# Turning the strided q and k of five batches by DMA transposes instead of TensorE transposes

## The chip, the cores and the metric

One core of a Trainium2 chip runs the whole program. The metric is the device time of one execution in microseconds (us). Executions of one kernel scatter by about 1%; where two traces of one kernel exist, they differ only at the start, where the first weights arrive (shown below). Every execution told here was in the fast state, but for micro, a single run whose state is unknown.

In this program TensorE does the matmuls and writes them to banks of PSUM. ScalarE and VectorE do the softmax and copy ("evict") the banks to SBUF, the on-chip memory. GpSimd casts loaded tiles to 16 bits, and SyncE issues the loads and stores. A DMA transpose is a transfer that turns a matrix on its way.

## The reference

Eight batches of causal attention with eight heads of 64 and 576 tokens, then a multiplicative feed-forward part over all 4608 tokens:

```python
mask_local   = (rel >= 0) & (rel < 32)                 # heads 0..3
mask_strided = (rel >= 0) & (k_pos % 32 == q_pos % 32) # heads 4..7
attn = softmax(where(mask, q @ k.T / 8, -1e9)) @ v
x = attn.transpose(0, 2, 1, 3).reshape(4608, 512)
out = ((x @ w1) * (x @ w2) @ w3) @ w_out               # 512 -> 1024 -> 512
```

## The kernel before

It is recorded as a list of operations that a small scheduler in the kernel's source orders at build time; each engine then runs its list in order. w3 @ w_out is folded into one matrix `w34` at the start. After that, nine tiles of 512 tokens (ps_a, ps_b, ps_o: `x @ w1`, `x @ w2`, `... @ w34`) alternate with the attention of the batches ahead of them. Two heads make a head pair; pairs 0 and 1 are local, 2 and 3 strided.

Scores need q and k with the 64 head elements on the partitions. So 512 of the 576 tokens come in as 128 rows of 4 tokens, are cast by GpSimd, turned by TensorE (ps_T) and copied out of PSUM; the other 64 "rest" tokens come in extra and are turned by small matmuls (ps_R):

```python
def fnT(e, ...):                       # one head pair: q and k, 8 transposes
    for j, x in ((0, "q"), (1, "k")):
        ps = bank("f", key)[:, j]
        for c in range(4):
            nc.tensor.transpose(ps[:, c*P:(c+1)*P], x16[(b, x, hp // 2)][:, c, h0:h0 + 2]..., id16)
tp = plan.op(key, {"PE": 450}, fnT, ...)
def fe(e, i, ...):                     # two evictions: into qT, and into kTL (local) or kTS (strided)
    copy(e, o, ps.rearrange(...))
evs.append(plan.op(f"E{nm}{nm2}", {"ACT": 590, "DVE": 690}, fe, deps=[tp] + wr, ...))
...
plan = Plan(dict(f=NF, B=2, stg=NSTG, asb=2, osb=3, ...))   # f: four PSUM banks; osb: three output buffers
# output: ScalarE copies a PSUM bank into an osb buffer, SyncE stores it; the buffer is free when that has landed
```

The softmax here doesn't subtract the row's maximum and nothing guards it: scores larger than these inputs give would overflow.

## Time and profile before

| | before |
|---|---|
| time, median of 4 runs | 279.55 us (278.8 to 280.18) |
| span of the profiled execution | 277.2 us |
| TensorE / VectorE / ScalarE / GpSimd busy | 97 / 63 / 63 / 43% |
| period of a tile while attention runs beside | 27.23 us |

The prediction shows the main lines: TensorE has no gap between about 40 us and the end. Two groups of the page (busy us and mean ns of one, then idle time before and who ended it) are what the change removes in part:

```profile
L666 PE MATMUL ps_T<-id,x 128*128 128x128 f16 x256 | 19.5, 219 | 1.0 <-POOL x L308 0.8
L304 ACT COPY qT<-ps_T 128x512 f16<-128x512 f16 x16 | 9.4, 588 | 9.3 <-PE ps_T L666 9.3
```

The 256 transposes are 32 blocks of eight; ten blocks go. What a block costs is worked out in the prediction.

### The profile page before, as it was taken

The numbers are of one execution on the slowest core, as the hardware profiler recorded it, in microseconds if no ns is written. First come the engines' busy times: TensorE is split into PE (matmuls) and PEld (weight loads), VectorE is DVE, ScalarE is ACT, GpSimd is POOL, SyncE is SP. The second block draws the span as 40 slices with busy tenths as digits, with TensorE's granted clock in tenths as the row PEclk, the third lists the DMA queues.
The fourth block names the chain that finished last, engine by engine and source line by source line (L and its number), as shares of the span: only waits on it lengthen the run. The fifth ranks groups of instructions, "written<-read, shape, count | busy, mean of one in ns | idle before, by whom it ended". The sixth has DMA issues, their size and how long they took to land.

```text
span 277.2 us, 6298 instructions
## 1 busy us (share of the span) xinstructions
PE 268.5 (97%) x2433; PEld 150.8 (54%) x2433; DVE 173.6 (63%) x328; ACT 174.1 (63%) x321; POOL 117.9 (43%) x146
## 2 busy tenths in 40 slices
PE   7977999999999999999999999999999999999995
PEld 3556885656555555555555555555555544444443
DVE  6544577776778577857785778577767763320321
ACT  2862477847668775886588668856885775324321
POOL 6676987699969969450835082100000000000000
PEclk9999999999999999999999999999999999999999
DMA  7999999998999998977366200310030003003003
GB/s 245 338 361 273 344 357 359 264 267 272 362 280 276 322 297 298 257 245 234 114 163 229 85 4 0 115 40 2 1 116 38 2 24 127 4 0 151 0 2 151
DMA packets 53422, 48.65 MB, mean 175 GB/s; under 512 B 20752, under 2 KB 45584, under 8 KB 53392
## 3 DMA queue, kind: packets, MB, share of 16 engines
q1 hardware_dynamic: 53392, 48.24, 57.3%
q8 instruction: 19, 0.31, 0.5%
q14 instruction: 11, 0.09, 0.1%
HBM read 38.80 MB, written 9.44 MB: 174 GB/s over the span
## 4 chain that ended last, share of the span: by engine, by line
PE 91%; DMA 6%; POOL 2%; SPq 0%; DVE 0%; issue 0%; DVEq 0%
PE ps_o L897 23%; PE ps_b L877 23%; PE ps_a L861 22%; PE ps_T L666 5%; PE ps_mm L594 4%; PE ps_S L709 4%; DMA st<-in_moe_w_out_dram 3%; PE ps_X L757 3%; PE ps_X L747 3%; DMA st<-in_k_dram 3%; PE ps_U L826 2%; PE ps_tr L575 1%; PE ps_R L619 1%; SPq L311 0%; POOL x16r L308 0%; POOL woh L308 0%
## 5 line engine op out<-in xcount | busy, mean ns | idle before, releaser
L883 DVE TENSOR_TENSOR abt<-ps_b,asb 128x512 f16<-128x512 f32 x72 | 49.3, 689 | 39.3 <-PE ps_b L877 38.7
L877 PE MATMUL ps_b<-xT,w2h 128*128 128x512 f16 x288 | 73.8, 379 | 0.0
L861 PE MATMUL ps_a<-xT,w1h 128*128 128x512 f16 x288 | 73.8, 379 | 0.0
L304 ACT COPY asb<-ps_a 128x512 f32<-128x512 f32 x72 | 42.2, 589 | 40.2 <-PE ps_a L861 39.4
L897 PE MATMUL ps_o<-w,abt 128*128 128x512 f16 (+1 forms) x296 | 67.4, 374 | 0.0
L308 POOL CAST x<-st 128x1024 f16<-128x1024 f32 x32 | 32.8, 1037 | 31.6 <-PE ps_T L666 25.2
L877 PEld LDWEIGHTS <-w2h 128*128 128x128 f16 x288 | 26.9, 98 | 29.2
L897 PEld LDWEIGHTS <-abt 128*128 128x128 f16 x296 | 26.9, 98 | 27.7
L861 PEld LDWEIGHTS <-w1h 128*128 128x128 f16 x288 | 26.5, 99 | 26.5
L727 ACT ACTIVATE ps_S<-ps_S 96x576 f32<-96x576 f32 (+1 forms) x56 | 32.9, 628 | 11.0 <-PE ps_S L709 10.5
L304 ACT COPY osb<-ps_o 128x512 f32<-128x512 f32 x35 | 20.6, 588 | 18.4 <-PE ps_o L897 18.2
L813 DVE TENSOR_TENSOR xT<-ps_X,rcp 64x288 f16<-64x288 f32 x56 | 25.1, 448 | 5.9 <-ACT rcp L797 5.3
L308 POOL CAST v16L<-st 32x768 f16<-32x768 f32 (+1 forms) x32 | 26.3, 821 | 3.0 <-DMA st<-in_v_dram 1.3
L735 DVE TENSOR_TENSOR ptm<-ps_S,maskL 128x576 f16<-128x576 f32 x28 | 19.8, 750 | 12.2 <-ACT ps_S L727 12.2
L776 DVE TENSOR_TENSOR xqs<-ps_X,rcq 96x384 f16<-96x384 f32 (+1 forms) x36 | 20.5, 568 | 1.2
L735 DVE TENSOR_TENSOR ptm<-ps_S,maskS 96x576 f16<-96x576 f32 x28 | 19.8, 748 | 1.3 <-ACT ps_S L727 0.5
L666 PE MATMUL ps_T<-id,x 128*128 128x128 f16 x256 | 19.5, 219 | 1.0 <-POOL x L308 0.8
L308 POOL CAST v16S<-st 96x1024 f16<-96x1024 f32 x16 | 16.4, 1035 | 6.0 <-PE ps_X L747 6.0
L797 ACT ACTIVATE rcp<-ps_X 64x576 f32<-64x576 f32 x28 | 18.1, 647 | 0.9
L786 ACT ACTIVATE ps_X<-ps_X 64x576 f32<-64x576 f32 x28 | 17.7, 631 | 0.9 <-PE ps_X L747 0.5
L666 PEld LDWEIGHTS <-x 128*128 128x128 f16 x256 | 15.5, 98 | 3.1 <-POOL x L308 1.3
L306 DVE COPY qT<-ps_T 128x512 f16<-128x512 f16 x16 | 11.1, 692 | 9.2 <-PE ps_T L666 9.2
(79 smaller groups left out, 276.6 us busy)
## 6 DMA issues: line engine op xcount, KB each, us to landing
out_dram<-osb SPq DMA_DIRECT2D x35, 256.0 KB
st<-in_moe_w_dram SPq DMA_DIRECT2D x16, 512.0 KB
st<-in_q_dram SPq DMA_DIRECT2D x16, 512.0 KB
st<-in_k_dram SPq DMA_DIRECT2D x16, 512.0 KB
st<-in_v_dram SPq DMA_DIRECT2D x16, 288.0 KB
st<-in_v_dram SPq DMA_DIRECT2D x16, 256.0 KB
st<-in_moe_w_out_dram SPq DMA_DIRECT2D x4, 512.0 KB
st<-in_q_dram SPq DMA_DIRECT2D x8, 128.0 KB
```

The costliest lines, as they stand in the source:

```text
L304: pin(nc.scalar.copy(out=out, in_=in_))
L308: pin(nc.gpsimd.tensor_copy(out=out, in_=in_))
L666: pin(nc.tensor.transpose(ps[:, c * P:(c + 1) * P], x16[(b, x, hp // 2)][:, c, h0:h0 + 2] .rearrange("p h d -> p (h d)"), id16))
L727: pin(nc.scalar.activation(out=sps, in_=sps, func=AF.Exp, bias=0.0, scale=scale))
L735: pin(nc.vector.tensor_mul(ptm[0:kr, 0:576].rearrange("p (h a x) -> p h a x", h=2, x=w), pte[0:kr].rearrange("p h (a x) -> p h a x", x=w), ...
L776: pin(nc.vector.tensor_mul(xqs[0:w, 0:m].rearrange("p i h d -> p h i d"), xv[:, :, :, 0:D], _ap(rcp, 0, [[rcp.ap[0][0], w], [4, 2], [1, m] ...
L797: pin(nc.scalar.activation(out=rcp, in_=i, func=AF.Exp, bias=0.0, scale=-1.0))
L813: pin(nc.vector.tensor_mul(o, i0, i1))
L861: pin(nc.tensor.matmul(ps, w1h[:, ci, js], xT[ci][:, tok], start=(ci == 0), stop=(ci == KM - 1)))
L877: pin(nc.tensor.matmul(ps, w2h[:, ci, js], xT[ci][:, tok], start=(ci == 0), stop=(ci == KM - 1)))
L883: pin(nc.vector.tensor_mul(big[("abt", t)][:, jc, :], bank("f", f"b{t}_{jc}"), live[("asb", t, jc)]))
L897: pin(nc.tensor.matmul(ps, big[("abt", t)][:, ci, bass.ds(ts * P, P)], w34[:, ci, bass.ds(pt * nw, nw)], start=(ci == 0), stop=(ci == KF - ...
```

## The change

Strided heads attend within one residue of 32, and a row of 8 tokens (72 rows for 576 tokens) keeps the 8 tokens at fixed places, so all 576 tokens fit one layout and DMA can turn it: 80x1024 float16 in SBUF (72 rows, padded to 80) become 128x8x80 in one instruction. Batches 3 to 7 do so for both strided pairs, four DMA transposes a batch, all issued by SyncE.

```diff
-        r += [("qk", b, 0), ("r", b), ("vL", b, 0), ("vL", b, 1), ("qk", b, 1), ("vS", b, 0), ("vS", b, 1)]
+        r += [("qk", b, 1)] if b < 3 else [("qs", b, 0), ("qs", b, 1)]     # cut
+            def ft(e, nm=nm):
+                o = (qT[:, hp] if nm == "q" else kTS[:, hh, 0:ST * SC]).rearrange("x (c w) -> x c w", w=SC)
+                pin(nc.sync.dma_start(o, x16[(b, nm, hp)].rearrange("p c h d -> p (c h d)"), transpose=True))
+            o = DTop[(b, nm, hp)] = plan.op(f"D{nm}{b}_{hp}", {"SP": 1300}, ft, deps=[c], dma=1700, store=True)
+            late.append((o, lambda: [Sop.get((b - 1, h)) for h in (2, 3)]))
 ...
+            if dt:
+                evs = [DTop[(b, nm, hp)] for nm in "qk"]     # the scores wait for the DMA, no ps_T, no evictions
-            for part in range(2):
+            for part in range(2 if b < LB else 1):           # no ps_R evictions for strided heads
 ...   # mask, loads of v and score offsets follow the 72-row layout; the scheduler books SyncE by each operation's own time; cut
```

More of the change, by code (lines that the diff above doesn't have):

```diff
@@ L32, in _loads @@
     for b in range(2, 8):
-        r += [("qk", b, 0), ("r", b), ("vL", b, 0), ("vL", b, 1), ("qk", b, 1), ("vS", b, 0), ("vS", b, 1)]
+        r += [("qk", b, 0), ("r", b), ("vL", b, 0), ("vL", b, 1)]
+        r += [("qk", b, 1)] if b < 3 else [("qs", b, 0), ("qs", b, 1)]
+        r += [("vS", b, 0), ("vS", b, 1)]
     return r
@@ L38 @@
            pord=lambda b: (2, 3, 0, 1) if b < 2 else (0, 1, 2, 3), tsplit=False, dmaf=1.08, nhr=8, cast=dict(w1=dict(POOL=1040)),
-           first=('DVE', 'ACT', 'POOL'), early=0, pm=4, nx=4, nstg=7, new=(2, 3))
+           first=('DVE', 'ACT', 'POOL'), early=0, pm=4, nx=4, nstg=7, new=(2, 3), lb=3)
 def _ap(t: bass.AP, off_add, dims):
@@ L151, in order @@
                         avail["SP"].remove(o)
-                        busy["SP"] = t + 450
-                        stream = max(stream, t + 450 + 300) + o.dma * self.DMAF
+                        busy["SP"] = t + o.eng["SP"]
+                        stream = max(stream, t + o.eng["SP"] + 300) + o.dma * self.DMAF
                         landed.append(stream + self.DMA_LAT)
@@ L328, in spin @@
         pin(nc.tensor.matmul(ps, w34[:, 0, 0:P], w34[:, 0, :], start=True, stop=True))
-    qT = consts.tile([P, 4, S], FP16)
+    LB = cfg.get("lb", B)
+    SC = 80
+    qT = consts.tile([P, 4, ST * SC], FP16)
     kTL = consts.tile([P, 2, 32 + S + 32], FP16)
@@ L448 @@
     w3c, woc, w1c, w2c, x16, x16op, vop = {}, {}, {}, {}, {}, {}, {}
-    Top, Rop, Sop, PVop = {}, {}, {}, {}
+    Top, Rop, Sop, PVop, DTop = {}, {}, {}, {}, {}
     late = []
@@ L541, in load_vL, with load_s, load_qs, fn @@
             vop[(b, hp, g)] = cs + [hl]
+    def load_s(key, ten, b, hh):
+        src = ten[b, 4 + 2 * hh:6 + 2 * hh].rearrange("h (p c) d -> p h (c d)", c=ST)
+        return dma(key, key, 830, [P, 2, ST, D], lambda s: s[0:SQ].rearrange("p h c d -> p h (c d)"), src, clean=2)
+    def load_qs(b, hh):
+        hp = 2 + hh
+        for nm, ten in (("q", q), ("k", k)):
+            key = f"{nm}s{b}_{hh}"
+            d = load_s(key, ten, b, hh)
+            def fn(e, nm=nm, key=key):
+                t = qkp.tile([SC, ST, 2, D], FP16, tag=f"{nm}1", name="xs16")
+                copy(e, t.rearrange("p c h d -> p h c d"), stg[key][0:SC])
+                x16[(b, nm, hp)] = t
+            c = cast("c" + key, key, [d], CE.get("qs", POOL), fn)
+            late.append((c, lambda nm=nm: [DTop[(b - 1, nm, hp)]] if b > LB else
+                         [Top.get((b - 2 + hh, h)) for h in (2, 3)]))
+            def ft(e, nm=nm):
[3 more added lines that the diff above has]
+            late.append((o, lambda: [Sop.get((b - 1, h)) for h in (2, 3)]))
     def load_vS(b, hp):
@@ L545, in load_vS @@
         key = f"vS{b}_{hp}"
+        if b >= LB:
+            ds = [load_s(key, v, b, hp)]
+            c = cast("c" + key, key, ds, CE.get("vS", POOL),
+                     lambda e: copy(e, vt[0:SQ, 2 * hp:2 * hp + 2, :, 0:D], stg[key][0:SQ]))
+            late.append((c, lambda: [PVop.get((b - 2, 2 + hp, g)) for g in (0, 1)]))
+            for g in range(2):
+                vop[(b, 2 + hp, g)] = [c]
+            return
         sv = v[b, 4 + 2 * hp:6 + 2 * hp].rearrange("h (p c) d -> p h (c d)", c=ST)
@@ L557 @@
     LOAD = {"wo": load_wo, "w3": load_w3, "w12": load_w12, "qk": load_qk, "r": load_rest, "vL": load_vL,
-            "vS": load_vS}
+            "vS": load_vS, "qs": load_qs}
     for it in cfg["loads"]:
@@ L632, in fn @@
                     elif i == 0:
-                        copy(e, qT[:, 2:4].rearrange("x g (s w) -> x g s w", w=SQ)[:, :, :, 64:SQ], pr[:, i, 2:4])
+                        copy(e, qT[:, 2:4, 0:S].rearrange("x g (s w) -> x g s w", w=SQ)[:, :, :, 64:SQ], pr[:, i, 2:4])
                     else:
@@ L646 @@
             m = n // 2
-            kr = P if local else KB
-            kT, kw = (kTL[:, hp], LQ) if local else (kTS[:, hp - 2], KB)
+            dt = b >= LB and not local
+            kr, mk = (P, maskL) if local else (SQ, maskK) if dt else (KB, maskS)
+            kT, kw, qw = (kTL[:, hp], LQ, w) if local else (kTS[:, hp - 2], SC if dt else KB, SC if dt else w)
             rank = lambda ph, b=b, pi=pi: cfg["arank"](b, pi, ph)
@@ L654 @@
             tp = None
-            for i, nm in enumerate("qk"):
+            if dt:
+                evs = [DTop[(b, nm, hp)] for nm in "qk"]
+            for i, nm in enumerate("qk" if not dt else ""):
                 key = f"T{nm if split else ''}{nm2}"
@@ L681, in fe @@
                     else:
-                        o = (qT[:, hp].rearrange("x (u c w) -> x u c w", u=2, c=4)[:, :, :, 0:64] if i == 0 else
+                        o = (qT[:, hp, 0:S].rearrange("x (u c w) -> x u c w", u=2, c=4)[:, :, :, 0:64] if i == 0 else
                              kTS[:, hp - 2, 0:ST * KB].rearrange("x (u c w) -> x u c w", u=2, c=4)[:, :, :, 32:KB])
@@ L688 @@
                                    give=[("f", key)] if split or i == 1 else [], rank=3))
-            Top[(b, hp)] = tp
+            if tp:
+                Top[(b, hp)] = tp
             norms = []
@@ L692, with fnS @@
             old = 4 * b + pi < cfg.get("nx", 0) or hp not in cfg.get("new", (2, 3))
-            def fnS(e, hp=hp, nm2=nm2, w=w, m=m, kT=kT, kw=kw, local=local, pm=pm):
+            def fnS(e, hp=hp, nm2=nm2, w=w, m=m, kT=kT, kw=kw, qw=qw, local=local, pm=pm):
                 for g in range(2):
@@ L705, in fnS @@
                     for i in range(m):
-                        ks, qs = kw * (g * m + i), w * (g * m + i)
+                        ks, qs = kw * (g * m + i), qw * (g * m + i)
                         for h in range(2):
@@ L730, with fm @@
                             give=[("B", sk)] if pm else [], rank=2)
-                def fm(e, sk=sk, kr=kr, local=local, n=n, w=w, pslot=pslot):
+                def fm(e, sk=sk, kr=kr, mk=mk, n=n, w=w, pslot=pslot):
                     ptm, pte = ptms[pslot], bank("B", sk)[:, :, 0:288]
-                    mk = maskL if local else maskS
                     pin(nc.vector.tensor_mul(ptm[0:kr, 0:576].rearrange("p (h a x) -> p h a x", h=2, x=w),
```

## The prediction

> **What bounds the kernel now.** I first read the totals by engine and the 40 slices of the page of the kernel before, to see whether one engine is the bound and in which stage.
>
> ```profile
> PE 268.5 (97%) x2433; PEld 150.8 (54%) x2433; DVE 173.6 (63%) x328; ACT 174.1 (63%) x321; POOL 117.9 (43%) x146
> PE   7977999999999999999999999999999999999995
> PEclk9999999999999999999999999999999999999999
> DMA  7999999998999998977366200310030003003003
> ```
>
> TensorE is busy 97% of 277.2 us at full clock; the next engines stand at 63%. The DMA engines are full up to about 125 us and then nearly idle, because loads run ahead of use. A busy TensorE is not yet a bound, so I asked for the stretches between the starts of consecutive output tiles.
>
> ```profile
> 125.60:152.83 27.23, 27.23 (x262) 14.93 (x260) 19.91 (x38) 19.78 (x38) 11.94 (x14) 1.00 0.61 188
> 152.83:180.06 27.23, 27.23 (x261) 14.91 (x260) 19.91 (x38) 19.78 (x38) 8.81 (x10) 1.00 0.13 47
> 180.06:207.28 27.22, 27.22 (x261) 14.93 (x260) 19.90 (x38) 19.77 (x38) 0.00 (x0) 1.00 0.11 40
> ```
>
> The columns are length, then busy time of TensorE, its weight loads, VectorE, ScalarE and GpSimd, then clock, DMA share and GB/s. TensorE fills each period wholly, and the period is the same to 0.01 us whether the DMA share is 0.61 or 0.11 and whether GpSimd works 11.9 us or not at all. So in this stage an instruction taken from TensorE shortens the time by its own spacing, and one taken from any other engine by nothing. The last step is what a block of transposes takes in that stream, read in the order of time of TensorE (start, duration, then the group):
>
> ```profile
> 145.60 0.42 PE L747 MATMUL ps_X<-ptm,v16S 96*128 96x72 f16 x8
> 145.85 0.61 PE L666 MATMUL ps_T<-id,x 128*128 128x128 f16 x8
> 146.31 0.42 PE L747 MATMUL ps_X<-ptm,v16S 96*128 96x72 f16 x8
> ```
>
> Durations of pipelined matmuls overlap, so I take starts: 146.31 - 145.85 = 0.46 us for the eight transposes of one head pair. Other blocks give 132.56 - 132.11 = 0.45. I use 0.45, not the 0.61 duration, nor the 19.5 us that the page books for all 256 transposes (0.61 a block), as that overlap is not time on the path.
>
> **What the Trainium skill says.** "TensorE: Matmul & The Clock Gate", section "Wait — 56ns, not 53.3ns?", gives a start-to-start of about 55.6 ns for warm matmuls of 128 columns; 0.45 us / 8 = 56 ns, so the trace agrees, and transposes have no hidden extra cost to win back. "VectorE: DVE Perf Modes", section "The three transpose paths", gives 1309 ns for one 128x128 transpose by DMA against 390 ns by TensorE: the new path is the slower one and pays only if it is hidden. "Advanced Engine Details and Errata", section "X-Bar Transpose (TRN2)", says that transposing DMAs are about as fast as plain ones (350 to 400 GB/s expected). "DMA: Bandwidth & Descriptors", section "Silent corruption: two transposing streams in flight at once", demands a single stream; here all transposes are issued from SyncE. The kernel before has no DMA transpose, so its trace can confirm none of the last three.
>
> **The change, part by part.**
>
> TensorE. The built order of instructions of the two kernels, compared, differs on TensorE by nothing but this: 80 transposes and their weight loads are gone (4868 rows against 4708), in ten blocks of eight, the two strided head pairs of batches 3 to 7; and one block of attention-times-v moved past one neighbour, five times. Local heads keep their transposes, and the small matmuls for the 64 rest tokens (ps_R) stay at eight a batch, as they also serve the local heads. Score matmuls keep 72 columns, attention-times-v keeps 72 columns with 72 in place of 96 contracted rows; neither changes the columns streamed, so I give them no gain. All ten removed blocks lie between 97 and 215 us, inside the stage where TensorE has no gap. Gain: 10 x 0.45 = 4.5 us.
>
> VectorE and ScalarE. Gone are 20 evictions of 128x512 at 0.59 us (ScalarE) or 0.69 us (VectorE), and 10 small evictions of ps_R (0.27 and 0.47 us): together about 15 us, nearly all ScalarE's. In the periods above each has over 7 us to spare, so none of this is on the path. It only loosens ScalarE.
>
> GpSimd. Per batch, two casts of 128x1024 become four of 80x1024. A cast's time follows its free size (96x1024 takes 1035 ns, 128x1024 1037 ns), so +2 x 1.04 us a batch, 10.4 us in all. In the stretches after 98 us it works 17.4, 11.9 and 8.8 us of 27; this hides.
>
> Loads. Strided q and k come as 2 KB rows (a row holds 8 tokens of 64 float32) instead of 1 KB; the rest tokens are still loaded. A batch moves 4 x 288 KB instead of 2 x 512 KB, 128 KB more, which at the some 300 GB/s of the loading stage is 0.4 us a batch of transfers that are well ahead.
>
> DMA transposes. Twenty of 80x1024 float16, 160 KB each, in 640 pieces of 256 B. Between 137.9 and 142.0 us mostly 256 B pieces of v were moved: 2309 packets in 4.1 us at a share of 0.702, that is 4.1 x 0.702 x 16 / 2309 = 20 ns of an engine per packet. 640 x 20 / 16 gives an estimate of 0.8 us of data time for one. Issue on SyncE is unknown; the changed kernel's own scheduler assumes 1.3 us to issue and 1.7 us to transfer. I take 1.3 for each issue and some 2 us until the last lands, so the four of a batch need about 4 x 1.3 + 2 = 7 us.
>
> Are they in time? They may start when the strided scores of the batch before are done, since qT and kTS have one buffer. In the period from 125.60 the last strided scores end at 143.6; the next batch's first strided scores start at 135.51 + 27.23 = 162.7, or 161.8 with two blocks gone between. That leaves 18 us for the first two transposes and some 26 for all four, against 7 needed. The first ones (batch 3) wait for scores that end at 89.3, and are needed at 107.4 (108.3 less two blocks): the same 18 us.
>
> Sum: 279.1 - 4.5 + 0 = 274.6. I add 0.3 us for small new waits and say 274.9.
>
> **The rivals.**
>
> First, SyncE as the new bottleneck. It issues in order, and the four transposes now stand ahead of the four output stores of a tile. Before, they left like this:
>
> ```profile
> 146.16 0.38 SPq L311 DMA_DIRECT2D st<-in_k_dram  x1
> 146.63 0.46 SPq L916 DMA_DIRECT2D out_dram<-osb  x1
> 147.38 2.82 SPq L311 DMA_DIRECT2D st<-in_v_dram  x4
> 150.30 3.06 SPq L916 DMA_DIRECT2D out_dram<-osb  x3
> ```
>
> With 1.3 us each the first store moves from 146.6 to about 149.3. It took about 2.7 us from the last store's issue (274.5) to the span's end, so that buffer is free at about 152. Output buffers are three; ScalarE's fourth copy stood at 152.42, so it is just met, and the two copies of ps_T that followed it are gone. If one transpose holds SyncE 2.5 us, the store leaves at 154, the fourth copy waits some 4 us, ScalarE's next copies queue behind it, and TensorE runs out of its four PSUM buffers after about three more blocks of 0.86 us: a loss near 2 us in each of five periods, 10 us against the gain, so 284 to 285. If one holds it 8 us, the scores themselves wait (two need 16 plus landing against 18, four 32 against 26) and the time passes 295. Against it: the skill's rate[...], and batches 0 to 2 being left out suggests a choice tuned to the busy DMA stage. For it: nothing in the trace before shows one transpose.
>
> Second, a load or cast that comes late. Casts of strided q and k of batch b now wait for the DMA transposes of batch b - 1, because the 16-bit tiles hold one batch, not two; and in-order SyncE, while it waits to transpose, issues no loads. For it: DMA share 0.93 from 98 to 125 us. Against it: GpSimd itself waits for TensorE there, up to 10.5 us at a time, so loads are over a batch ahead. For instance the local q and k of batch 7 now stand behind batch 5's transposes, which start at about 142; they are needed near 193. I give this 0 to 2 us.
>
> Third, a larger gain, if VectorE or ScalarE secretly paced TensorE. The periods without any TensorE gap speak against it; with all of the 10 x 0.61 us of booked time it would be 273.0. I give it little.
>
> **Range and chances.** Below 274.6 there is only rounding and the spread of the runs before (278.8 to 280.2), so the low end is 273.7. Upward lies the store delay; a partial form of it, 1 us in each of five periods, gives 279.6, so 279.5 is the high end. Faster by over 2% means below 273.5, 1.1 us more than all that TensorE gives up: 0.06. Slower by over 2% means above 284.7, the full form of the first rival: 0.10. Within 2%: 0.84.
>
> **What would show it.** Right: TensorE busy near 263 us with 80 fewer matmuls; four periods near 26.3 us (two blocks less) with no idle TensorE; transposes that start right after the last strided scores and land over 8 us before the next; no wait of scores on qT or kTS by DMA; ScalarE's output copies not waiting for stores. Wrong: idle TensorE after the third output block of a tile, with output copies waiting for out_dram (first rival, slow issue); scores waiting for a DMA transpose (slow transfer); TensorE waiting for a cast (second rival). What would break the prediction is a transpose that holds SyncE over 2 us.

## The result, and the profile after

Measured: 275.21 us median (274.92 to 276.59, 4 runs), ratio to before 0.9856 (95% interval 0.9811 to 0.99). Ratios here are the mean time of one kernel's fast runs over that of the other's in the same rounds, so they differ a little from the ratio of quoted medians. In a second call, five runs gave 275.36 us, ratio 0.9839 (0.9819 to 0.986). The prediction was 274.9, its bare sum 274.6. It is a small gain, within the 2% class that was given 0.84.

Totals and slices of the page of the changed kernel:

```profile
PE 263.9 (96%) x2353; PEld 145.8 (53%) x2353; DVE 173.7 (63%) x328; ACT 161.9 (59%) x291; POOL 128.4 (47%) x156
PE   7977899999999999999999999999999999999995
DMA  7999899989998998979999999932141012003004
```

TensorE lost 80 matmuls and 4.6 us. GpSimd gained 10.5 us, ScalarE lost 12.2, VectorE stayed as it was. The DMA row is the surprise: the engines are now full to about 178 us, where they were full to 125.

Stretches between the starts of consecutive tiles of the changed kernel (columns as in the prediction):

```profile
99.51:125.84 26.33, 26.33 (x246) 14.05 (x245) 19.93 (x38) 17.35 (x32) 15.39 (x18) 1.00 0.94 230
125.84:152.17 26.33, 26.33 (x246) 14.03 (x245) 19.93 (x38) 17.45 (x32) 15.22 (x19) 1.00 1.08 240
152.17:178.50 26.33, 26.33 (x246) 14.05 (x245) 19.90 (x38) 17.36 (x32) 17.55 (x20) 1.00 0.98 237
```

The period fell from 27.23 to 26.33 us, 0.90 for two blocks, and TensorE still fills all of it, although the DMA share rose from 0.13 to 0.98 in the stretch that starts at about 152 us. How a block leaves the stream is seen in the order of time of TensorE, first before, then after (start, duration, group):

```profile
151.34 1.04 PE L897 MATMUL ps_o<-w,abt 128*128 128x512 f16 x4
152.22 0.61 PE L666 MATMUL ps_T<-id,x 128*128 128x128 f16 x8
152.66 0.59 PE L861 MATMUL ps_a<-xT,w1h 128*128 128x512 f16 x2
```

```profile
151.29 1.04 PE L938 MATMUL ps_o<-w,abt 128*128 128x512 f16 x4
152.16 1.03 PE L902 MATMUL ps_a<-xT,w1h 128*128 128x512 f16 x4
```

From ps_o to ps_a it was 152.66 - 151.34 = 1.32 us and is 0.87: 0.45 less, with nothing in the place.

A table that I made from the traces shows where each kernel gains or loses: the start of the first ps_a of tile 0, and the distances from tile to tile.

```
              tile 0 at   0->1   1->2   2->3   3->4   4->5   5->6   6->7   7->8
before           41.10   29.44  27.67  27.23  27.22  27.23  27.23  25.18  20.72
after            41.98   30.30  27.23  26.33  26.32  26.33  26.33  24.72  20.72
after_again      42.60   29.43  27.22  26.33  26.33  26.33  26.32  24.73  20.72
pe_back          41.48   29.42  27.23  27.22  27.22  27.22  27.22  25.62  20.72
ev_back          42.62   29.43  27.22  26.75  26.33  26.32  26.33  24.73  20.72
lb5              41.97   29.43  27.67  27.22  26.78  26.34  26.32  24.73  20.72
lb5_again        41.31   29.43  27.67  27.22  26.78  26.33  26.33  24.73  20.72
lb2              41.81   29.43  26.32  26.33  26.33  26.32  26.33  24.73  20.72
dt_small         41.35   29.63  27.22  28.41  28.81  27.98  28.09  24.73  20.72
dt_twice         41.52   29.50  27.23  30.49  33.69  29.67  33.26  24.73  20.72
v1               42.24   29.59  26.49  26.49  26.50  26.48  26.49  24.73  20.72
v3               42.06   29.60  26.49  26.49  25.96  26.52  26.51  24.23  21.29
v4               41.19   29.39  26.30  26.29  26.29  26.30  26.29  24.73  20.72
```

From tile 1 on, before to after loses 0.44 + 4 x 0.90 + 0.46 = 4.5 us. The two profiled spans differ by 2.7 us only, because this execution reached tile 0 0.9 us later and spent 0.9 us more in tile 0. That is scatter: after_again, the same program, took 29.43 us there. The first tile begins between 41.1 and 42.6 us over the traces, and two traces of one kernel (after, after_again; lb5, lb5_again) differ by 0.6 to 0.7 us there. So an effect below 1 us is better read from the periods than from the times.

The SyncE queue of the changed kernel during one batch's transposes:

```profile
144.77 2.29 SPq L568 DMA_TRANSPOSE qT<-xs  x1
147.11 1.44 SPq L568 DMA_TRANSPOSE kTS<-xs  x1
148.65 3.99 SPq L568 DMA_TRANSPOSE qT<-xs  x1
152.70 1.27 SPq L568 DMA_TRANSPOSE kTS<-xs  x1
154.06 0.54 SPq L957 DMA_DIRECT2D out_dram<-osb  x1
```

Here the first output store of the tile leaves at 154.06 us. The prediction had put it at about 149.3, and 154 into the rival that costs 10 us. Yet the list of waits has only this for all output copies on ScalarE (us in total, times, longest):

```profile
ACT osb L306 <- DMA out_dram<-osb: 0.9, 2, 0.6
```

ScalarE's order of time offers the reason. The fourth output copy, before and after:

```profile
152.42 0.59 ACT L304 COPY osb<-ps_o 128x512 f32<-128x512 f32 x1
158.44 0.59 ACT L306 COPY osb<-ps_o 128x512 f32<-128x512 f32 x1 [0.64 <-DMA out_dram<-osb]
```

The scheduler reckons 1.3 us of SyncE for each transpose and gives an output buffer out only when it reckons its store landed, so it put the fourth copy behind the next tile's first work. Meanwhile one of four PSUM banks stays taken for six microseconds, and TensorE has no gap for it. No run puts the copy back to its old place, so that the order averts the loss is argued from the trace.

### The profile page after: what moved, and what is told of

It is laid out like the page before. It is cut to its first block, busy times and chain, and to the rows that moved or that the text cites. A ratio compares the mean times of both kernels' runs of the same rounds, so it can differ in the third digit from the quotient of the medians.

```text
span 274.5 us, 6186 instructions
## 1 busy us (share of the span) xinstructions
PE 263.9 (96%) x2353; PEld 145.8 (53%) x2353; DVE 173.7 (63%) x328; ACT 161.9 (59%) x291; POOL 128.4 (47%) x156
## 4 chain that ended last, share of the span: by engine, by line
PE 89%; DMA 6%; POOL 2%; ACT 1%; SPq 1%; DVE 0%; issue 0%; DVEq 0%; POOLq 0%
PE ps_o L938 23%; PE ps_b L918 23%; PE ps_a L902 22%; PE ps_mm L632 4%; PE ps_S L751 4%; DMA st<-in_moe_w_out_dram 4%; PE ps_X L798 3%; PE ps_T L707 3%; PE ps_X L788 3%; DMA st<-in_k_dram 2%; PE ps_U L867 2%; PE ps_tr L613 1%; PE ps_R L657 1%; SPq L313 1%; ACT ps_S L769 0%; POOL x16r L310 0%
## 5 line engine op out<-in xcount | busy, mean ns | idle before, releaser
L769 ACT ACTIVATE ps_S<-ps_S 128x576 f32<-128x576 f32 (+2 forms) x56 | 32.8, 626 | 10.5 <-PE ps_S L751 9.9
L310 POOL CAST x<-st 128x1024 f16<-128x1024 f32 x22 | 22.7, 1037 | 13.7 <-DMA st<-in_k_dram 7.9
L776 DVE TENSOR_TENSOR ptm<-ps_S,maskL 128x576 f16<-128x576 f32 x28 | 19.8, 751 | 12.2 <-ACT ps_S L769 12.2
L310 POOL CAST xs<-st 80x1024 f16<-80x1024 f32 x20 | 20.1, 1034 | 5.9 <-DMA qT<-xs 2.4
L310 POOL CAST v16S<-st 72x1024 f16<-72x1024 f32 (+1 forms) x16 | 16.4, 1035 | 11.6 <-DMA st<-in_v_dram 11.3
L798 PEld LDWEIGHTS <-ptm 128*96 128x96 f16 (+1 forms) x224 | 14.5, 123 | 5.5 <-issue 0.2
L632 PE MATMUL ps_mm<-woh,w3T 128*128 128x256 f16 x128 | 15.9, 272 | 1.4 <-POOL woh L310 1.3
```

The source lines that it names most:

```text
L310: pin(nc.gpsimd.tensor_copy(out=out, in_=in_))
L632: pin(nc.tensor.matmul(ps, big[f"w3T{kc // 4}"][:, kc % 4, js], big["woh"][:, kc, ns], start=(kc == 0), stop=(kc == KF - 1)))
L769: pin(nc.scalar.activation(out=sps, in_=sps, func=AF.Exp, bias=0.0, scale=scale))
L776: pin(nc.vector.tensor_mul(ptm[0:kr, 0:576].rearrange("p (h a x) -> p h a x", h=2, x=w), pte[0:kr].rearrange("p h (a x) -> p h a x", x=w), ...
L798: pin(nc.tensor.matmul(xps[0:w, h, i * 65:(i + 1) * 65], ptms[pslot][0:kr, c0:c0 + w], vt[0:kr, 2 * (hp % 2) + h, g * m + i, 0:D + 1], sta ...
```

## The experiments

Twelve further runs were made. The first forms of two of them (ev_back, dt_twice) did not fit into SBUF and were rebuilt with their unused results in a weight buffer that is free by then. All but micro gave the right result.

**pe_back and ev_back: which of the removed parts was the gain?**

```diff
+                if not local and kw == SC:                       # pe_back, ahead of the strided scores
+                    for i in range(8):
+                        pin(nc.tensor.matmul(bank("B", f"S{nm2}_{i % 2}")[:, 0, 0:P], id16, id16, start=True, stop=True))
```
```diff
+        for j in range(2):                                       # ev_back, on ScalarE, after the third asb copy and the fourth output copy of a tile
+            copy(e, big["junk"][:, j * NM:(j + 1) * NM], xT[0][:, 0:NM])
```

> The changed kernel, with 8 unused matmuls of 128 columns put back on TensorE ahead of each of the ten strided score groups that are fed by DMA transposes; nothing else differs, and the order of everything else is the same. Theory A (the gain is the time of ten blocks of eight transposes on a TensorE that has no gap): 10 x 0.45 = 4.5 us come back, about 279.5 us, ratio to the kernel before 1.00. Rival B (the gain came from the evictions or the loads that went away): the 80 matmuls fill waits, 275 to 276 us, ratio 0.985 to 0.99.

Measured: 280.01 us, ratio 1.0016 (0.9998 to 1.0034). The periods are back at 27.22. Theory A holds, rival B falls.

> The changed kernel, with 20 copies of 128x512 float16 put back on ScalarE at the places where the 20 evictions stood (some 12 us of ScalarE work), results unused. Theory A: ScalarE has over 7 us to spare in a period, so about 275.2 us, ratio 0.985. Rival B (relief of ScalarE made the gain): about 279 us, ratio 1.00.

Measured: 275.96 us, ratio 0.9866 (0.9834 to 0.9898). Twenty copies cost one period 0.4 us and the others nothing. So ScalarE's relief was at most a small part of the gain. The expectation says that the copies stand where the evictions stood. That isn't so for the half that is tied to the fourth output copy, which had moved: in one tile the pairs stand at 158.36 and 159.87 us, where the kernel before had them at 152.90 and 159.99. The ten small evictions of ps_R were not put back.

**lb5 and lb2: does the gain grow with the batches?**

```diff
-... if b < 3 else ...   lb=3
+... if b < 5 else ...   lb=5      # lb2: 2
```

> The change for batches 5 to 7 only (six blocks of transposes gone instead of ten). Theory A, 0.9 us a batch: 279.5 - 2.7 = 276.8 us, ratio 0.990. A rival in which the gain is made in the full-DMA stage (2 KB rows of q and k): next to nothing is left, 279 us.

Measured: 278.29 us over 21 runs (277.01 to 279.46), ratio 0.9944 (0.9927 to 0.9962). This misses the 0.990 expected: half of the expected gain was not there in those runs, though the trace has every period as expected.

> The same kernel as lb5, which came out at 278.3 us where 276.8 was expected, while its traced execution (275.4 us) showed every tile period as expected and only a first tile 0.9 us later. If the 1.4 us are an accident of those runs' start: about 277 us, ratio 0.990 to 0.992. If something in this kernel loses time in most runs: 278.3 again, and a trace of a slow execution should show TensorE idle outside the start.

Measured: 277.35 us, ratio 0.9914 (0.9897 to 0.9932), on another chip. It is near what was expected, and the new trace again has the expected periods. What the first 21 runs lost is not in a trace, so it stays open; differences at the start are the only ones that any two traces of one kernel show.

> The change for batches 2 to 7 (twelve blocks gone). Theory A, if the transposes of batch 2 hide as well: 279.5 - 5.4 = 274.1 us, ratio 0.981. If the stage before 70 us, where the DMA engines are full and TensorE waits for loads at the start, can't carry four more transposes: 275 us or more, with TensorE idle before about 80 us in the trace.

Measured: 274.59 us, ratio 0.9817 (0.9788 to 0.9846). Period 1->2 fell from the changed kernel's 27.23 to 26.32 as well, TensorE has no gap after the start, and four more transposes beside full DMA engines cost nothing. So the prediction's thought that batches 0 to 2 were left out to suit the busy DMA stage is not borne out for batch 2. This is 0.7 us under the changed kernel by the medians of separate calls, where two blocks by 0.45 give 0.9.

**after_again**

> The changed kernel once more beside the others, five rounds: 275.2 us, ratio 0.984 to 0.986 if the gain is ten blocks of 0.45 us.

Measured: 275.36 us, ratio 0.9839, as expected.

**micro: what does one DMA transpose cost alone?**

```diff
+    # lines shortened
+    for i in range(20): nc.sync.dma_start(dst[i % 8], x16a[0:80, :], transpose=True)        # 80x1024
+    for i in range(20): nc.sync.dma_start(pie[i % 8][:, :, 0:128], xb[0:80, :]...)          # 256 B pieces, plain
+    for i in range(20): nc.sync.dma_start(row[i % 8], xc[0:80, :])                          # 2 KB rows, plain
+    for i in range(20): nc.sync.dma_start(sml[i % 8], xd[0:96, 0:384], transpose=True)      # 96x384
```

> Wrong result on purpose (a tile of zeros and a few other values is stored). With nothing else running: 20 DMA transposes of 80x1024 float16 back to back, then 20 plain copies of the same bytes within SBUF in 256 B pieces, 20 in 2 KB rows, and 20 transposes of 96x384. If a transpose moves bytes like a plain transfer of 256 B pieces, as the prediction estimated: 0.8 us each. If the extra DMA time in the changed kernel's trace (some 35 us of all engines over 20 transposes) is the transposes': 1.7 us each, twice the plain copy or more.

The SyncE queue of this kernel (start, time for all twenty):

```profile
5.22 26.49 SPq L39 DMA_TRANSPOSE dT<-x16a  x20
34.45 15.60 SPq L52 DMA_DIRECT2D dP<-x16b  x20
53.84 12.66 SPq L55 DMA_DIRECT2D dR<-x16c  x20
69.93 26.19 SPq L58 DMA_TRANSPOSE dU<-x16d  x20
```

And its stretches inside the first two phases (last columns: clock, DMA share, GB/s):

```profile
6.00:32.00 26.00, 0.00 (x0) 0.55 (x4) 0.00 (x0) 1.00 0.65 122
36.00:49.00 13.00, 0.00 (x0) 0.00 (x0) 0.00 (x0) 1.00 0.98 205
```

Alone, a transpose holds SyncE 26.49 / 20 = 1.32 us, and one with under half the data just as long (1.31). The engines' own time is 0.65 x 1.32 = 0.86 us, close to the 0.78 us (15.60 / 20) of the plain copy in 256 B pieces. So the prediction's 0.8 us of data time was right for a transpose alone, and the other hypothesis, 1.7 us each, falls there: of the additional DMA time in the changed kernel (0.708 x 274.5 - 0.573 x 277.2 = 35 us of all engines, by the shares and spans of the two pages) twenty transposes explain 20 x 0.86 = 17 us. The kernel also has the strided loads in another shape and everything running at once; which of these fills the engines is not settled. A full DMA share is also not full speed: 0.98 and 1.08 went with 237 and 240 GB/s there, and 0.93 with 265 before.

**dt_twice and dt_small: how much more turns the gain into a loss, and is it SyncE's time or the data?**

```diff
+                # dt_twice: all of it once more, into an unused tile
+                pin(nc.sync.dma_start(jk[n % 3][:, 0:ST * SC].rearrange("x (c w) -> x c w", w=SC),
+                                      x16[(b, nm, hp)].rearrange("p c h d -> p (c h d)"), transpose=True))
+                # dt_small instead: an eighth of it
+                pin(nc.sync.dma_start(jk[n % 3][:, 0:SC], x16[(b, nm, hp)][:, 0].rearrange("p h d -> p (h d)"), transpose=True))
```

> The changed kernel with each of the 20 DMA transposes issued twice, the first time into an unused tile; the order of the rest is the same. It doubles what SyncE holds (8 x 1.25 = 10 us a batch) and the data moved. If the transposes are hidden with the slack that the trace shows (first pair landed some 10 us before the scores): TensorE waits little, 275.2 to 278 us, ratio under 0.995. If the prediction's first rival is right about its threshold (2.5 us per transpose costs 2 us in each of five periods by late output stores): 284 to 285 us, ratio 1.02, with output copies waiting for out_dram and idle TensorE after the third output block.

Measured: 296.92 us, ratio 1.0609 (1.0588 to 1.063). My expectation of slack was wrong; the loss is there, and larger than the rival said. The waits of ScalarE's output copies, and one stretch:

```profile
ACT osb L306 <- DMA out_dram<-osb: 21.2, 4, 7.1
128.74:162.43 33.69, 29.42 (x245) 14.94 (x244) 19.89 (x38) 17.34 (x32) 15.86 (x19) 0.90 1.02 208
```

The columns are those of the prediction. The period of 33.69 us has 33.69 - 29.42 = 4.27 us of idle TensorE, and the same matmuls take 29.42 instead of 26.33 us, at a mean clock of 0.90. So the wait is paid 1.7 times. The Trainium skill, "TensorE: Matmul & The Clock Gate", section "What's actually happening", has TensorE's clock halve after an idle window of about 3.4 us. The traces agree for the most part: waits of 4.27 and 4.54 us come with a clock of 0.90 in their stretch, those of 3.18 us and of dt_small (at most 2.31 us) with 1.00. But one of 1.93 us came with 0.94: in stretches of 1 us the clock is 0.50 from 108 to 110 us, after that wait, as it is from 141.8 to 148 us after the one of 4.27. So it halves as the page says, but the length of a wait alone does not decide it here.

> As dt_twice (296.9 us), but the additional transpose turns only 80x128 of the 80x1024, an eighth of the bytes. In the run micro a transpose of 96x384 held SyncE as long (1.31 us) as one of 80x1024 (1.32 us). If the issue time on SyncE is what made dt_twice slow and it is the same for any size: 290 us or more, with output copies waiting for out_dram. If the moved data on the full DMA engines did it, or if the issue of a small one is short: 275 to 279 us.

Measured: 283.35 us, ratio 1.0129 (1.0098 to 1.0161), between the two expectations. An 80x128 transpose holds SyncE about as long as a full one (columns: minimum, median and maximum ns):

```profile
L572 SPq DMA_TRANSPOSE junk<-xs x20: 1104/1220/2751, 89.2 to 204.4; - x20
```

What it does is the same chain with shorter waits, in the orders of time of ScalarE and TensorE:

```profile
137.12 0.58 ACT L306 COPY osb<-ps_o 128x512 f32<-128x512 f32 x1 [4.11 <-DMA out_dram<-osb]
```

```profile
137.75 1.02 PE L908 MATMUL ps_a<-xT,w1h 128*128 128x512 f16 x4 [2.31 <-ACT osb L306]
```

ScalarE waits 4.11 us for an output buffer, then TensorE 2.31 us for ScalarE. So holding SyncE about 2.5 us per transpose, with little more data, costs 283.35 - 275.36 = 8.0 us, near the 10 us and 284 to 285 us of the first rival (1.7 to 2.5 us in each of four periods, where it said near 2 us in five). The other 13.6 us of dt_twice come with the seven eighths of data that dt_small leaves out, and with the clock.

**v1, v3 and v4: further along the lever.** v1 is lb2 that also stops loading and turning the rest tokens of the strided heads, which nobody reads in these batches:

```diff
+                    if b >= LB:     # 32 columns instead of 64, over 64 partitions; v4: x16[...][:, i, c], idR2[0:KB]
+                        pin(nc.tensor.matmul(pv[:, i, 0:4, c], x16[(b, "r")][0:64, i, c]..., idR2[0:64], ...))
```

> A further step along the same lever: the change for batches 2 to 7, and for these batches the rest tokens of the strided heads are no longer loaded nor turned on TensorE (ps_R streams 32 columns instead of 64, eight a batch). Twelve blocks: 279.6 - 5.4 = 274.2 us as lb2 showed (274.6); halving 8 x 64 columns saves at most [...]0.1 us a batch, 0.6 us in all: 274.0 us. A rival: a matmul of 32 columns takes no less than one of 64 columns with its weight load: 274.6.

Measured: 275.87 us, ratio 0.986, 1.3 us worse than lb2. The periods are 26.49 us and not 26.33. (The 0.1 us a batch of the expectation is an estimate; at the 56 ns that 128 columns take in the stream, 256 columns are 0.11 us.) TensorE in order of time:

```profile
142.54 1.04 PE L947 MATMUL ps_o<-w,abt 128*128 128x512 f16 x4
143.51 0.36 PE L663 MATMUL ps_R<-idR,x16r 64*128 64x32 f16 x8
143.81 1.04 PE L947 MATMUL ps_o<-w,abt 128*128 128x512 f16 x4
```

143.51 - 142.54 = 0.97 us instead of the 0.87 of four such matmuls, and the block takes 0.30 us. In lb2, whose blocks contract over 96 partitions, these are 0.87 and 0.24 us (starts at 141.62, 142.49 and 142.73). To contract over 64 partitions between matmuls over 128 cost 0.1 us at entry, and fewer columns saved nothing.

> v1 with ps_R contracted over 96 partitions (32 of them zero rows of the identity) instead of 64; nothing else differs. In v1's trace a tile period was 26.49 us where lb2's was 26.33: the 0.1 us wait of TensorE ahead of ps_R, as ahead of the 64-row scores, and 0.06 us more for the block itself. If the 64-row contraction made both: periods of 26.2 to 26.33 us, some 274 to 274.6 us, ratio 0.980 to 0.982. If 32 columns are slow by themselves: 26.4 to 26.5 us, as v1.

Measured: 274.73 us, ratio 0.9824 (0.9805 to 0.9844). The block takes 0.21 us, the period is 26.29. The 64-row contraction was the fault, and half the columns are worth about 0.04 us a period. By the times v4 and lb2 are the same.

v3 is v1 that also turns the local heads' output by DMA from batch 4:

```diff
+                    pin(nc.sync.dma_start(xT[hp][:, S*b:S*b + S].rearrange("x (t w) -> x t w", w=LQ), xqd[0:LQ, 0:LT*P]..., transpose=True))
```

> v1, and from batch 4 the eight local head pairs also turn their normalized output by one DMA transpose of 96x768 each instead of six TensorE transposes (ps_U, 0.26 us a pair by starts) and a copy. On TensorE 8 x 0.26 = 2.1 us less than v1: 272 us, if the two more transposes a batch (2.6 us of SyncE) leave the output stores and loads in time. If SyncE is now too full: output copies waiting for out_dram and idle TensorE, 274 us or more.

Measured: 275.56 us, ratio 0.9858. Eight blocks of ps_U are gone, but only two periods fell by the expected 0.5 us. In two others ps_o waits 0.37 us for ScalarE, and in the last tile but one a ps_a waits 0.40 us for VectorE's last write of the attention's output (20.72 became 21.29). No output copy waits for a store, so the stated rival is not what happened. The order of work changed as well, and I did not settle which part of it used up the gain.

## Why the prediction was right

- **The bound and the price of a block.** Ten blocks by 0.45 us from starts, 4.5 us. The periods show 0.90 for two blocks, pe_back gives all of it back, and in the traces the sums from tile 1 on scale with it: 2.7 us less for six blocks (lb5), 4.5 for ten, 5.4 for twelve (lb2). Using the booked 0.61 us a block would have given 273.0, which was not reached.
- **ScalarE and VectorE off the path.** Right but for at most 0.4 us, by the periods and ev_back. The size was off: I summed durations to about 15 us, and ScalarE lost 12.2, since its copies overlap, as the matmuls do (starts 152.42 and 152.90 us, 0.59 us each).
- **GpSimd +10.4 us, hidden.** 10.5 measured; no TensorE wait on a cast after the start.
- **The data time of 0.8 us.** 0.86 by micro.
- **Transposes in time.** Right: in the shown batch the first pair is issued by 148.55 us and its scores come at 161.78, and no scores wait for a DMA.
- **Four transposes in 7 us, first store at 149.3.** This step was mis-sized: in the shown batch they took from 144.77 to 153.97, as one of them held SyncE 3.99 us while loads filled the DMA engines, and the store left at 154.06. Why one waits so long is not shown; alone, twenty in a row took 1.32 us each, and a plain load at 139.30 us held SyncE 2.09 us as well. The prediction's own sign of being broken, a transpose that holds SyncE over 2 us, thus came (2.29 and 3.99 us; the four took 2.3 on average), and the time was met all the same. What saved the result, as far as the trace shows it, is not the argument that I gave (a buffer "just met" at 152.42) but the order: the scheduler had put the fourth copy later. I had read the copy's old place in the trace of before and not its new place in the built order. For this step the right total was luck.
- **The first rival.** Its price holds at about 2.5 us a transpose (dt_small, 8.0 us). Its premise alone, a first store at 154 us, cost nothing in the changed kernel. It left out the clock, which falls in dt_twice.
- **Loads ahead.** Right in result: no wait of TensorE. But I had 0.4 us a batch of additional transfer, and the DMA engines stayed full 50 us longer.

## What to carry to other kernels

Where one engine has no gap, as here, an instruction taken from it was worth its start-to-start distance in the stream (0.45 us a block); read that from two neighbours, not from its duration. Work moved to DMA was free only as long as nothing that stood behind it in the issuing queue came late: count the issue time and find what stands next in that queue. In the built order, look up where the waiting instruction will stand, not where it stood.

## What the Trainium skill lacked or had wrong

- "VectorE: DVE Perf Modes", section "The three transpose paths": it gives 1309 ns for a 128x128 DMA transpose, which reads as a price per block. Here it is a nearly fixed time on the issuing engine: 1.22 us for 80x128, 1.31 for 96x384, 1.32 for 80x1024. No page gives this time for a transpose within SBUF on this chip ("DMA: Bandwidth & Descriptors" has sequencer cycles of "previous generations" only, beside trn3); a plain store's issue took 0.33 us in the kernel before.
- "Advanced Engine Details and Errata", section "X-Bar Transpose (TRN2)": 350 to 400 GB/s and "as fast as regular DMAs"; at 350 GB/s the 160 KB would take about 0.5 us, an estimate, which the prediction held against its first rival. Issued from one queue at 160 KB each, the runs show 122 GB/s; plain SBUF copies of the same bytes gave 205 (256 B pieces) and 243 GB/s (2 KB rows). Only the engines' own time is alike.
- "TensorE: Matmul & The Clock Gate", section "Part 4: PE-mode transpose": some 275 ns a transpose in a kernel and 390 alone. Both read as the duration of one, which is 219 ns here; the section lacks what one costs in a stream: eight take 0.45 us, 56 ns each, at full clock.
- "TensorEngine Tiling (Array Packing)", section "Tiling Modes", says that a change of tiling mode drains TensorE but gives no figure. In v1, TensorE lost 0.1 us where a contraction over 64 partitions followed one over 128 (0.97 instead of 0.87 us); that this is that drain is not shown.
